# Attention weights that change partitions by DMA through a DRAM scratch instead of on GpSimd, and a bank of their own for block 0's scores

## The chip, the cores and the metric

One Trainium2 chip, and of it one core. The metric is the device time of one execution in microseconds; the number compared is the median over runs. TensorE (PE in profiles) multiplies matrices, VectorE (DVE), ScalarE (ACT) and GpSimd (POOL) do the elementwise work, and SyncE (SP) issues nearly all DMAs. PSUM, into which TensorE writes, has eight banks of 128 partitions x 512 f32.

## The reference

Windowed causal attention (8 batches, 8 heads, 576 positions, head size 64, window 64) gives 4608 tokens of 512 features; they go through an RMS norm and a gated MLP with 1536 hidden features.

```python
scores = scale * np.matmul(q, k.transpose(0, 1, 3, 2))
mask = (rel >= 0) & (rel < window)
scores = np.where(mask, scores, -1000000000.0)
attn = np.exp(scores - np.max(scores, axis=-1, keepdims=True))
attn = attn / (np.sum(attn, axis=-1, keepdims=True) + 1e-09)
x = (attn @ v).transpose(0, 2, 1, 3).reshape(4608, 512)
xn = x / np.sqrt(np.mean(x * x, axis=-1, keepdims=True) + 1e-06) * rms_g
g = xn @ w_gate
out = (g * sigmoid(g) * (xn @ w_val)) @ w_out
```

## The kernel before

Tokens are worked on in nine tiles of 512. The MLP's matmuls are in f16, each f32 operand split into a high and a low half, three matmuls for one product. Tiles 0 to 2 run plainly (`expert_in`, L794 to L796 and L843 to L846). Tiles 3 to 8 (`all_sevens`, L922) form a 2 x 2 block product from seven products instead of eight: for each of six chunks of hidden features the products 1, 5, 2, 6, 3, 7 and 4 stand at the slots of the table PLACE, 66 slots a tile, with output groups (six matmuls of L794 to L796 into a bank `po`) in slots that are free. Product 4 of a chunk adds into the bank of product 1, and so waits until VectorE has taken product 7's sum out of it (L982). Its weights come from a scratch in DRAM, `sevens`, through `load_sevens` (L895 to L904): three sets of four SBUF tiles `wt`, one set a chunk, loaded three chunks ahead as soon as the chunk that used the set is through its product 4. The sevens themselves are made during tiles 1 and 2 (L870 to L884, the halves `hi` and `lo` going out to DRAM over SP).

Attention is worked on by pairs of heads, n = 0 to 31, four a batch. Batches 0 and 1 turn their weights with matmuls. The 24 pairs from n = 8 on are spread over the MLP by `visit(n)`, whose places are numbers in half steps (32 a tile): the table VISITS for the first, then every 8. A visit does two things on TensorE. First come the scores of pair n (`quarter`, L389): nine blocks, eight of 128 columns into two banks `sc_n_0` and `sc_n_1`, and block 0, of 64 columns, into the tail (from column XSPLIT = 320) of a bank `x0_n`. Then come the values of pair n-2 (`attention_values`, L511): the first five blocks into columns 0 to 319 of that same bank `x0_n`, the other four into one more bank, `xp`.

The scores leave PSUM on VectorE: `masked` (L402), block 0 first, writes them with the mask added to the SBUF tile `pm_n` and keeps their extreme in `st_n`; ScalarE takes the exponentials (`weigh`, L405) and the sums; VectorE forms the reciprocals (L431, L432). The weights must then be turned so that keys lie on partitions. That takes two steps. POOL's `move` (L374) carries 32-row blocks between groups of partitions and multiplies by the reciprocal on the way, 16 instructions a pair, in four parts that are due 4 to 8.7 half steps after the visit and 0.8 apart (MOVES); VectorE's `turn` (L377, L378) transposes the 32 x 32 blocks, due three half steps before visit n+2. Two tiles' halves of `pm_n` serve as source and target. In the same time the values of finished pairs are squared and summed (L579), and at the end of a batch normalised: inverse roots on VectorE (L692 to L699), scaling (L744), splitting into halves on ACT and POOL (L777, L778, with VectorE's L783 to L789).

What sets the order: TensorE's order is that of the program from tile 1 on. The other engines' queues, SP's among them, are put in order by a scheduler when the kernel is built, on a timeline that it estimates; on the chip each queue then runs strictly in order. After tile 2 all eight banks of PSUM are handed out in rotation (`any_bank`); before that block 0's bank comes from a small pool.

## Time and profile before

| | |
|---|---|
| median of 3 runs | 1045.39 us (1043.51 to 1045.95) |
| the profiled execution | 1047.58 us |
| its span, first to last instruction | 1045.8 us |
| mean granted clock of TensorE | 0.97 |
| busy: PE, DVE, ACT, POOL | 975.9, 668.9, 510.6, 543.1 us |
| TensorE's first instruction of tile 1, 2, 3, 4 | 210.97, 348.2, 459.0, 561.5 us |
| visits' scores of pairs 18, 22, 26, 30 | 447.7, 550.2, 656.6, 762.0 us |
| DMA bytes | 143.42 MB |

Rows of the profile read: line, engine, operation, tiles out<-in, count, busy us, then the idle time ahead of them and what ended it. A wait row gives the line that waited and the line that released it, the us in all, the times and the longest. A timeline row begins with the start in us from the span's start and the duration.

### The profile page before, as it was taken

How to read it: one execution, taken by the hardware profiler on the slowest of the kernel's cores; microseconds unless marked ns; L12 is line 12 of the kernel's file. 1: busy time of each engine (PE TensorE's matmuls, PEld its weight loads, DVE VectorE, ACT ScalarE, POOL GpSimd, SP SyncE). 2: the span in 40 equal slices, each digit the busy share in tenths (PEclk: the TensorE clock that was granted, in tenths of full speed). 3: DMA queues.
4: the chain of work that ended last, by engine and by line, in shares of the span. 5: the costliest groups of instructions: out<-in, count | busy, mean ns of one | idle time of the engine just before them, and what ended most of it. 6: DMA issues, size and time to landing. Idle time of an engine off the chain costs nothing.

```text
span 1045.8 us, 20545 instructions
## 1 busy us (share of the span) xinstructions
PE 975.9 (93%) x7751; PEld 632.9 (61%) x7751; DVE 668.9 (64%) x1713; ACT 510.6 (49%) x1303; POOL 543.1 (52%) x679
## 2 busy tenths in 40 slices
PE   7889989998978999989998999899989999999998
PEld 5544544543433454468755885588558847866875
DVE  5688956377869744856686668666876666531550
ACT  5557885254522444256535654565346525532541
POOL 3326633579866666766666666666666404200210
PEclk9989989999989899999998999999999999999999
DMA  7647961222220444136632664266325523641501
GB/s 284 193 139 216 269 187 46 76 95 97 88 86 30 157 141 144 55 97 217 210 114 87 218 204 138 87 213 206 130 75 179 177 89 96 207 152 54 189 2 41
DMA packets 71331, 143.42 MB, mean 137 GB/s; under 512 B 25024, under 2 KB 25280, under 8 KB 71232
## 3 DMA queue, kind: packets, MB, share of 16 engines
q1 hardware_dynamic: 70656, 140.93, 42.3%
q8 instruction: 61, 1.00, 0.4%
q10 hardware_dynamic: 576, 1.18, 0.3%
q14 instruction: 38, 0.31, 0.1%
HBM read 121.64 MB, written 20.45 MB: 136 GB/s over the span
## 4 chain that ended last, share of the span: by engine, by line
PE 58%; DVE 18%; POOL 12%; ACT 7%; issue 3%; DMA 2%; SPq 0%; POOLq 0%; DVEq 0%; ACTq 0%
PE a L922 26%; POOL pm L374 10%; PE po L794 6%; PE po L795 6%; PE po L796 6%; DVE xb L744 3%; PE sc L389 2%; ACT pm L405 2%; DVE r L697 2%; DVE r L698 2%; PE xp L511 2%; DVE r L699 2%; PE x L511 2%; DVE pm L377 1%; PE pv L794 1%
## 5 line engine op out<-in xcount | busy, mean ns | idle before, releaser
L374 POOL TENSOR_TENSOR pm<-pm,st 32x288 f32<-32x288 f32 (+1 forms) x384 | 267.8, 697 | 115.1 <-DVE st L432 45.6
L922 PEld LDWEIGHTS <-wt 128*128 128x128 f16 x3024 | 295.8, 98 | 42.9 <-issue 2.2
L922 PE MATMUL a<-xn,wt 128*128 128x256 f16 x1728 | 203.8, 274 | 1.2 <-ACT ot L1041 0.8
L795 PE MATMUL po<-wt,h 128*128 128x512 f16 (+1 forms) x436 | 165.0, 378 | 0.0
L794 PE MATMUL po<-wt,h 128*128 128x512 f16 (+1 forms) x436 | 164.7, 378 | 0.0
L796 PE MATMUL po<-wt,h 128*128 128x512 f16 (+1 forms) x436 | 164.6, 378 | 0.0
L954 POOL TENSOR_TENSOR h<-th,h 128x512 f16<-128x512 f32 x60 | 69.1, 1159 | 154.5 <-ACT h L953 139.3
L922 PE MATMUL a<-wt,wt 128*128 128x256 f16 x1224 | 146.2, 273 | 0.0
L405 ACT ACTIVATE pm<-pm,st 128x128 f32<-128x128 f32 (+1 forms) x216 | 83.2, 387 | 21.8 <-DVE st L402 21.6
L947 DVE SCALAR_TENSOR_TENSOR th<-th,a 128x256 f32<-128x256 f32 x108 | 45.3, 419 | 65.1 <-ACT th L946 65.0
L946 ACT ACTIVATE th<-a,hsc 128x256 f32<-128x256 f32 x108 | 51.3, 475 | 52.6 <-PE a L922 29.8
L953 ACT CAST h<-th 128x512 f16<-128x512 f32 x72 | 44.4, 617 | 63.4 <-DVE th L948 63.4
L796 PEld LDWEIGHTS <-h 128*128 128x128 f16 x436 | 43.1, 99 | 49.4 <-issue 2.2
L794 PEld LDWEIGHTS <-h 128*128 128x128 f16 x436 | 43.3, 99 | 46.9 <-issue 3.0
L795 PEld LDWEIGHTS <-h 128*128 128x128 f16 x436 | 43.1, 99 | 46.0 <-issue 3.4
L794 PE MATMUL pv<-xn,wt 128*128 128x512 f16 x144 | 57.6, 400 | 8.9 <-DVE th L843 8.9
L389 PE MATMUL sc<-kv,q 64*64 64x128 f32 (+1 forms) x1056 | 56.5, 296 | 8.1 <-DMA q<-q 5.1
L777 ACT CAST xn<-xb 128x192 f16<-128x192 f32 (+7 forms) x33 | 12.9, 423 | 101.7 <-DVE xb L744 101.5
L377 DVE STREAM_TRANSPOSE pm<-pm 128x1024 f32<-128x1024 f32 x24 | 29.8, 1243 | 48.1 <-POOL pm L374 48.1
L975 DVE TENSOR_TENSOR a<-a,s 128x512 f32<-128x512 f32 x36 | 25.0, 696 | 54.7 <-PE a L922 54.6
L778 POOL TENSOR_TENSOR xn<-xb,xn 128x192 f16<-128x192 f32 (+7 forms) x33 | 28.3, 877 | 58.1 <-ACT xn L777 57.7
L511 PE MATMUL x<-pm,kv 128*64 128x64 f32 (+1 forms) x480 | 26.1, 250 | 34.7 <-DVE st L402 34.7
(184 smaller groups left out, 1831.2 us busy)
## 6 DMA issues: line engine op xcount, KB each, us to landing
wt<-sevens SPq DMA_DIRECT2D x108, 512.0 KB, 3.8
kv<-kv SPq DMA_DIRECT2D x28, 608.0 KB, 4.7
wt<-sevens SPq DMA_DIRECT2D x36, 256.0 KB, 3.7
q<-q SPq DMA_DIRECT2D x28, 288.0 KB, 3.0
kv<-kv SPq DMA_DIRECT2D x56, 128.0 KB, 4.8
out<-ot SPq DMA_DIRECT2D x27, 256.0 KB, 2.0
st<-w_gate SPq DMA_DIRECT2D x6, 1024.0 KB, 6.4
st<-w_val SPq DMA_DIRECT2D x6, 1024.0 KB, 5.9
```

The lines of the kernel that those rows point to most:

```text
L374: nc.gpsimd.tensor_tensor(m[to, :us, fr], p[fr, :us, to], r, ALU.mult)
L389: nc.tensor.matmul(out.rearrange("p (n c) -> p n c", c=D), lhsT=qt[hd, j * D : (j + 1) * D], rhs=halves[hd, :1, :] if j == 0 else halves[h ...
L405: nc.scalar.activation(part, part, AF.Exp, bias=low, scale=-1.0, accum_out=total)
L511: nc.tensor.matmul(xp[hd, c * D : (c + 1) * D], lhsT=vv[j][rows, hd], rhs=w, start=True, stop=True, skip_group_check=True,)
L794: nc.tensor.matmul(acc, lhsT=lh, rhs=rh, start=first, stop=False)
L795: nc.tensor.matmul(acc, lhsT=lh, rhs=rl, start=False, stop=False)
L796: nc.tensor.matmul(acc, lhsT=ll, rhs=rh, start=False, stop=last)
L922: nc.tensor.matmul(acc[:, i * HT : (i + 1) * HT], lhsT=ws[l][:, kt, :], rhs=b[:, m, kt, :], start=at_start, stop=kt == 1 and j == 2, skip_ ...
L946: nc.scalar.activation(cols, acc[:, :HT], AF.Tanh, scale=th_scale[:, c : c + 1])
L947: nc.vector.scalar_tensor_tensor(cols, cols, 1.0, acc[:, :HT], ALU.add, ALU.mult)
L953: nc.scalar.copy(hh, th)
L954: (nc.vector if c == NC - 1 else nc.gpsimd).tensor_tensor(hl, th, hh, ALU.subtract)
```

## The change

It has three parts. Block 0's scores get a bank `s0_n` of their own; in tiles 0 to 2 it comes from the pool with one bank that other small results use too. The move between partitions leaves POOL: for a pair, two multiplies over all 128 partitions by the reciprocals (128 x 1024 and 128 x 64), a memset, then on SP four DMA writes of 144 KB, one for each group of 32 partitions, into a scratch `via` in DRAM, and one read of 576 KB back into the other half of `pm_n`. For this the weights lie as [partition, 32-column block k, key block j, 32]. The moves are due 1.5 half steps after the visit and the transposes 6. Last, `load_sevens` loads a chunk's weights with two DMAs (1024 and 768 KB) in place of four, and two small buffers lose their second copy to make room.

```diff
@@ -40,13 +40,13 @@
 VISITS = (27, 32, 37, 42.5, 47.5)
-MOVES = (8.7, 7, 4.5, 4)
+MOVED, TURNED = 1.5, 6
 FIRST7 = 3
 PREP0, PREP1 = 34.0, 72.0
-ST = 2 * NBLK * P - D
+ST = 2 * NBLK * P - 32
 NRB = 2
@@ -101,7 +101,8 @@
-    wt = [cp.tile([P, 2, 1024], F16, name=f"wt{i}") for i in range(3 * NC + 2)]
+    wts = [cp.tile([P, 4, 2, 1024], F16, name=f"wt{i}") for i in range((3 * NC + 2) // 4)]
+    wt = [w[:, i] for w in wts for i in range(4)]
@@ -359,23 +360,29 @@
         t = wk.tile([P, ST], I32, tag="st8", name=f"pm_{n}", bufs=NST).bitcast(F32)
-        return (t[:, a : a + NBLK * P].rearrange("p (j k) -> p j k", k=P) for a in (0, ST - NBLK * P))
+        return (t[:, a : a + NBLK * P].rearrange("p (k j c) -> p k j c", k=4, j=NBLK) for a in (0, ST - NBLK * P))
-    def move(m, p, rs, k):
-
-        us = NBLK - 1 if k > 1 else NBLK
+    def move(n, m, p, rs):
+
+        for ks, us in ((4, slice(0, NBLK - 1)), (2, slice(NBLK - 1, NBLK))):
+            r = rs[:, us].rearrange("p (a j b) -> p a j b", a=1, b=1).to_broadcast([P, ks, us.stop - us.start, 32])
+            nc.gpsimd.tensor_tensor(p[:, :ks, us, :], p[:, :ks, us, :], r, ALU.mult)
+        nc.gpsimd.memset(p[:, 2:, NBLK - 1, :], 0.0)
+        via = dram.tile([P, 4, NBLK * 32], F32, tag="via", name=f"via_{n}", bufs=3)
         for qq in range(4):
-            fr, to = slice(32 * qq, 32 * qq + 32), slice(32 * k, 32 * k + 32)
-            r = rs[fr, :us].rearrange("p (a b) -> p a b", b=1).to_broadcast([32, us, 32])
-            nc.gpsimd.tensor_tensor(m[to, :us, fr], p[fr, :us, to], r, ALU.mult)
+            nc.sync.dma_start(
+                out=via[:, qq, :].rearrange("(k i) c -> i k c", k=4),
+                in_=p[32 * qq : 32 * qq + 32].rearrange("i k j c -> i k (j c)"),
+            )
+        nc.sync.dma_start(out=m.rearrange("p q j c -> p q (j c)"), in_=via)
     def turn(p, m):
-        nc.vector.transpose(p[:, : NBLK - 1, :], m[:, : NBLK - 1, :])
-        nc.vector.transpose(p[0:D, NBLK - 1, :], m[0:D, NBLK - 1, :])
+        nc.vector.transpose(p[:, :, : NBLK - 1, :], m[:, :, : NBLK - 1, :])
+        nc.vector.transpose(p[0:D, :, NBLK - 1, :], m[0:D, :, NBLK - 1, :])
@@ -423,11 +430,12 @@
             w, v = P if u else D, slot(u)
-            masked(p[:, v, :w], place[u] if u else first[:, :D], blocked[:, :P] if u else blocked[:, P:],
-                   st[:, 0, v : v + 1])
+            src, hide = (x.rearrange("p (k c) -> p k c", c=32) for x in (
+                (place[u], blocked[:, :P]) if u else (first[:, :D], blocked[:, P:])))
+            masked(p[:, : w // 32, v, :], src, hide, st[:, 0, v : v + 1])
         for u in order:
             w, v = P if u else D, slot(u)
-            weigh(p[:, v, :w], st[:, 0, v : v + 1], st[:, 1, v : v + 1])
+            weigh(p[:, : w // 32, v, :], st[:, 0, v : v + 1], st[:, 1, v : v + 1])
         nc.vector.tensor_scalar(st[:, 1, :], st[:, 1, :], 1e-9, None, ALU.add)
@@ -507,9 +515,10 @@
                 i, par = divmod(j - 1 - 4 * g, 2)
-                w = at(1 + 4 * g + 2 * h + i)[:, par * D : (par + 1) * D] if j else at(0)[rows, hd]
+                w = at(1 + 4 * g + 2 * h + i, rows, par) if j else at(0, rows, h)
+                o = xp[hd, c * D : (c + 1) * D]
                 nc.tensor.matmul(
-                    xp[hd, c * D : (c + 1) * D],
+                    o if len(w.shape) == 2 else o.rearrange("p (a b) -> p a b", b=32),
                     lhsT=vv[j][rows, hd],
@@ -538,9 +547,9 @@
-        def moved(hp, k):
+        def moved(hp):
             p, m, rs = whole[b * NPAIR + hp]
-            move(m, p, rs, k)
+            move(b * NPAIR + hp, m, p, rs)
@@ -556,9 +565,9 @@
                 place = {u: p[h][:, i, :] for h in range(2) for i, u in enumerate(units(g, h))}
-                at = place.get
+                at = lambda u, rows, a: place[u][rows, a * D : (a + 1) * D]
             else:
-                at = lambda u: p[:, slot(u), :]
+                at = lambda u, rows, a: p[rows, 2 * a : 2 * a + 2, slot(u), :]
             xp = attention_values(n, g, at, vv, xp)
@@ -597,9 +606,8 @@
                 events.append((i0 - 7, partial(load_keys, hp)))
-                for k in range(4):
-                    events.append((i0 + (MOVES[hp] + 0.8 * k if n > 11 else 3.5 + 0.4 * k), partial(moved, hp, k)))
-                events.append((visit_at(n + 2) - half_steps * (b - 1) - 3, partial(turned, hp)))
+                events.append((i0 + MOVED, partial(moved, hp)))
+                events.append((i0 + TURNED, partial(turned, hp)))
                 visits[n] = partial(score, hp, 0), partial(values, hp)
@@ -623,7 +631,7 @@
         if n in visits:
-            visits[n][0](xp[:, XSPLIT:])
+            visits[n][0](any_bank(f"s0_{n}") if shared else ps_mi.tile([P, TT], F32, tag="mi", name=f"s0_{n}"))
         if n - 2 in visits:
@@ -896,12 +904,9 @@
             return
-        src = sevens[r % NC]
-        for j in range(4):
-            n = 2048 if j < 3 else 1024
-            nc.sync.dma_start(
-                out=wt[4 * (r % 3) + j].rearrange("p a n -> p (a n)")[:, :n], in_=src[:, 2048 * j : 2048 * j + n]
-            )
+        dst = wts[r % 3].rearrange("p i a n -> p (i a n)")
+        for a, z in ((0, 8 * TT), (8 * TT, 14 * TT)):
+            nc.sync.dma_start(out=dst[:, a:z], in_=sevens[r % NC][:, a:z])
```

What it moves on the queues is shown at three places. Lines of the changed kernel are 5 to 9 higher.

TensorE at visit 22, at the end of tile 3. `x_22` is the bank x0, `xp_1` the bank of the other values, `s_22` block 0's own bank, `sc_0` and `sc_1` the other scores, `po_3` an output group, `a_4_0` the first product of tile 4. Before:

```order
L389 MATMUL x_22_5748<-kv_5542,q_5540 64x64 x2
L389 MATMUL sc_0_5749<-kv_5542,q_5540 64x128
L389 MATMUL sc_1_5750<-kv_5542,q_5540 64x128
...
L511 MATMUL xp_1_5804<-pm_5152,kv_4873 64x64 x8
L794 LDWEIGHTS h_2_4758
L794 MATMUL po_3_5731<-wt_95,h_2_4758 128x512
...
L511 MATMUL x_22_5748<-pm_5152,kv_4873 64x64 x10
L794 LDWEIGHTS h_3_4948
L794 MATMUL po_3_5731<-wt_96,h_3_4948 128x512
```

And after:

```order
L396 MATMUL s_22_5642<-kv_5446,q_5444 64x64 x2
L396 MATMUL sc_0_5643<-kv_5446,q_5444 64x128
L396 MATMUL sc_1_5644<-kv_5446,q_5444 64x128
...
L520 MATMUL x_22_5641<-pm_5056,kv_4787 64x64 x10
L520 MATMUL xp_1_5698<-pm_5056,kv_4787 64x64 x8
...
L802 MATMUL po_3_5628<-wt_84,h_2_4671 128x512
...
L802 MATMUL po_3_5628<-wt_84,h_3_4869 128x512
```

The values into `x_22` moved ahead of `xp` and of one output group, directly behind the scores, and no longer write into a bank that holds scores. The later rows of TensorE are the same in both.

VectorE behind visit 22, at the first products of tile 4. `a_4_0` are the banks of those products, `th_0_0` and `th_0_1` the gate's tiles, `wt_92` and `wt_83` the tile into which product 7's sum is taken (L982, L987), `pm_5769` and `pm_5663` the weights of pair 22. Before:

```order
L432 RECIPROCAL st_5770<-st_5770 128x9
L975 TENSOR_TENSOR a_4_0_5877<-a_4_0_5877,s_4_0_5855 128x512
L947 SCALAR_TENSOR_TENSOR th_0_0_5891<-th_0_0_5891,a_4_0_5877 128x256
L948 SCALAR_TENSOR_TENSOR th_0_0_5891<-a_4_0_5877,th_0_0_5891 128x256
L978 TENSOR_TENSOR a_4_0_5863<-a_4_0_5863,s_4_0_5907 128x512
L947 SCALAR_TENSOR_TENSOR th_0_0_5891<-th_0_0_5891,a_4_0_5863 128x256
L948 SCALAR_TENSOR_TENSOR th_0_0_5891<-a_4_0_5863,th_0_0_5891 128x256
L982 TENSOR_TENSOR wt_92<-a_4_0_5842,wt_92 128x512
L377 STREAM_TRANSPOSE pm_5769<-pm_5769 128x1024
L947 SCALAR_TENSOR_TENSOR th_0_1_5965<-th_0_1_5965,wt_92 128x256
L378 STREAM_TRANSPOSE pm_5769<-pm_5769 64x128
```

And after:

```order
L440 RECIPROCAL st_5664<-st_5664 128x9
L980 TENSOR_TENSOR a_4_0_5772<-a_4_0_5772,s_4_0_5741 128x512
L952 SCALAR_TENSOR_TENSOR th_0_0_5786<-th_0_0_5786,a_4_0_5772 128x256
L953 SCALAR_TENSOR_TENSOR th_0_0_5786<-a_4_0_5772,th_0_0_5786 128x256
L983 TENSOR_TENSOR a_4_0_5749<-a_4_0_5749,s_4_0_5802 128x512
L384 STREAM_TRANSPOSE pm_5663<-pm_5663 128x4x256
L952 SCALAR_TENSOR_TENSOR th_0_0_5786<-th_0_0_5786,a_4_0_5749 128x256
L385 STREAM_TRANSPOSE pm_5663<-pm_5663 64x4x32
L953 SCALAR_TENSOR_TENSOR th_0_0_5786<-a_4_0_5749,th_0_0_5786 128x256
L987 TENSOR_TENSOR wt_83<-a_4_0_5728,wt_83 128x512
```

The two transposes of pair 22 moved ahead of the sum L987 (L982 before), by three rows.

SP around visit 24, inside tile 4. `wt` from `sevens` are weight loads, `kv` and `q` the inputs of later pairs. Before:

```order
L902 DMA wt_81<-sevens_143 128x2048
L902 DMA wt_82<-sevens_143 128x2048
L324 DMA q_7143<-q 128x576
L902 DMA wt_83<-sevens_143 128x2048
L902 DMA wt_84<-sevens_143 128x1024
L902 DMA wt_85<-sevens_144 128x2048
L902 DMA wt_86<-sevens_144 128x2048
L339 DMA kv_6545<-kv 128x1216
L352 DMA kv_6545<-kv 64x512
L353 DMA kv_6545<-kv 64x512
L902 DMA wt_87<-sevens_144 128x2048
L902 DMA wt_88<-sevens_144 128x1024
```

And after, with `via` the scratch and `pm_6334` the weights of pair 24:

```order
L909 DMA wt_81<-sevens_128 128x4096
L325 DMA q_6997<-q 128x576
L909 DMA wt_81<-sevens_128 128x3072
L377 DMA via_6473<-pm_6334 32x4x288 x3
L340 DMA kv_6413<-kv 128x1216
L353 DMA kv_6413<-kv 64x512
L354 DMA kv_6413<-kv 64x512
L377 DMA via_6473<-pm_6334 32x4x288
L909 DMA wt_82<-sevens_129 128x4096
L381 DMA pm_6334<-via_6473 128x1152
L909 DMA wt_82<-sevens_129 128x3072
```

The four writes wait for POOL's multiply and the read for the writes; what stands behind them in the queue is issued after them. A weight load waits for TensorE to be done with its tile, and one stands between the last write and the read.

More of the change, by code (lines that the diff above doesn't have):

```diff
@@ L296, in out_split @@
     def out_split():
-        mx = wk.tile([P, 1], F32, tag="mo1", name="omx")
+        mx = wk.tile([P, 1], F32, tag="mo1", name="omx", bufs=1)
         nc.vector.tensor_tensor(w_sq, w_sq, h_inv, ALU.mult)
@@ L684, in inverse_roots @@
             )
-        rm = wk.tile([P, 3, nst], F32, tag="rm", name=f"rm_{b}")
+        rm = wk.tile([P, 3, nst], F32, tag="rm", name=f"rm_{b}", bufs=1)
         m, r, w = (rm[:, i, :] for i in range(3))
```

## The prediction

> **What bounds the kernel now.** I read the page first, then the waits of TensorE by stage, the windows with the granted clock, the timeline round one visit, and last the DMA landings. The page's first row says that TensorE is the engine that sets the time; what it does not do is 7% of the span.
>
> ```profile
> PE 975.9 (93%) x7751; PEld 632.9 (61%) x7751; DVE 668.9 (64%) x1713; ACT 510.6 (49%) x1303; POOL 543.1 (52%) x679
> ```
>
> TensorE's waits, first from 211 to 346 us (tile 1), then from 346 to 880 us (tiles 2 to 6). Columns: total us, times, longest.
>
> ```profile
> PE x L511 <- DVE st L402: 14.5, 4, 6.9
> PE pv L794 <- DVE th L843: 6.1, 2, 3.9
> ...
> PE x L511 <- DVE st L402: 20.1, 9, 4.5
> ```
>
> Nearly all that TensorE waits for after 211 us is one thing: the values of pair n-2 (L511) go into the bank in which block 0's scores of pair n still stand, and VectorE's mask (L402) has not read them yet. Behind the long waits the granted clock falls. The windows give busy us of PE, PEld, DVE, ACT and POOL, then the clock; the first two rows are tile 1 and a later tile.
>
> ```profile
> 211.00:346.00 135.00, 114.31 (x787) 56.04 (x787) 108.74 (x257) 58.79 (x181) 100.13 (x114) 0.92 0.26 87
> 565.00:670.00 105.00, 99.57 (x942) 73.59 (x941) 73.19 (x195) 54.58 (x156) 67.22 (x90) 0.98 0.50 159
> ...
> 297.80:304.60 6.80, 5.24 (x31) 2.77 (x32) 5.31 (x26) 4.55 (x21) 0.00 (x0) 0.50 0.29 84
> 338.70:345.50 6.80, 4.68 (x40) 2.96 (x41) 5.69 (x25) 4.82 (x21) 1.16 (x1) 0.50 0.72 252
> 451.40:454.80 3.40, 3.40 (x39) 2.42 (x40) 1.55 (x16) 3.40 (x16) 1.55 (x3) 0.50 0.73 238
> 557.20:564.00 6.80, 6.49 (x38) 3.92 (x39) 4.95 (x25) 6.24 (x25) 4.83 (x7) 0.50 0.41 130
> 663.00:666.40 3.40, 3.33 (x25) 1.96 (x26) 3.40 (x17) 3.12 (x12) 3.40 (x4) 0.50 0.27 69
> 768.80:772.20 3.40, 3.40 (x25) 1.63 (x20) 3.37 (x17) 2.59 (x10) 3.40 (x4) 0.50 0.44 119
> 256.80:263.60 6.80, 5.14 (x13) 1.83 (x13) 5.70 (x9) 1.85 (x4) 5.99 (x8) 0.50 0.52 171
> ```
>
> Seven stretches at half clock: 20.4 us of them in tile 1 (three of 6.8), 17.0 us later (3.4 + 6.8 + 3.4 + 3.4). Half of each is lost work. So after 346 us 20.1 + 8.5 = 28.6 us hang on that bank, and in tile 1 14.5 + 6.1 + 10.2 = 30.8 us hang on VectorE being late (108.7 of 135 us busy there, against 73 of 105 later).
>
> **The change part by part: block 0's own bank.** It removes the wait at L511 itself. What is late next is read at visit 22, at the end of tile 3. Every tile end after 346 us has this form; the waits at the other three stand in the last rows.
>
> ```profile
> 532.19 0.21 DVE L432 RECIPROCAL st<-st 128x9 f32<-128x9 f32 x1
> 532.57 12.73 POOL L374 TENSOR_TENSOR pm<-pm,st 32x288 f32<-32x288 f32 x16 [8.61 <-ACT kv L574]
> 535.53 0.75 DVE L697 TENSOR_TENSOR r<-r 128x256 f32<-128x256 f32 x1
> 545.50 1.23 DVE L377 STREAM_TRANSPOSE pm<-pm 128x1024 f32<-128x1024 f32 x1
> 550.25 0.27 PE L389 MATMUL x<-kv,q 64*64 64x64 f32 x2
> 550.27 0.49 DVE L697 TENSOR_TENSOR r<-r 128x320 f32<-128x320 f32 x1
> 551.38 0.69 PE L511 MATMUL xp<-pm,kv 128*64 128x64 f32 x16
> 557.23 0.22 DVE L402 CUSTOM_DVE_ANT_0 pm<-x,blocked 128x64 f32<-128x64 f32 x1
> 557.51 1.53 PE L511 MATMUL x<-pm,kv 64*64 64x64 f32 x20 [4.04 <-DVE st L402]
> 561.51 2.70 PE L922 MATMUL a<-xn,wt 128*128 128x256 f16 x12
> 562.19 0.21 DVE L432 RECIPROCAL st<-st 128x9 f32<-128x9 f32 x1
> 565.34 1.47 PE L922 MATMUL a<-wt,wt 128*128 128x256 f16 x12
> 566.65 1.47 PE L922 MATMUL a<-xn,wt 128*128 128x256 f16 x12
> 576.05 1.25 DVE L377 STREAM_TRANSPOSE pm<-pm 128x1024 f32<-128x1024 f32 x1 [0.67 <-POOL pm L374]
> 578.42 3.77 PE L922 MATMUL a<-xn,wt 128*128 128x256 f16 x33
> ...
> 451.32 0.99 PE L511 MATMUL x<-pm,kv 64*64 64x64 f32 x10 [2.37 <-DVE st L402]
> 663.07 1.21 PE L511 MATMUL x<-pm,kv 64*64 64x64 f32 x14 [4.31 <-DVE st L402]
> 768.16 1.09 PE L511 MATMUL x<-pm,kv 64*64 64x64 f32 x20 [4.50 <-DVE st L402]
> ```
>
> Count from the scores, 550.25 = 0. With a bank of its own TensorE goes on: values at half of 1.53 us, the second bank's 0.6, two output groups of 1.3 (what lies between the first product of tile 4 and the one at 565.34 is one group, with a matmul's tail), so tile 4 begins at about +5.1 instead of +11.3. By the order its next gates are the bank of block 0's scores (second product, behind one more output group, +7.7; the mask is read at +7.2) and sc's bank (+9.0, when four masks of 0.2 us are done too). They are met almost without a wait. The five shorter waits after 346 us (20.1 less 2.37, 4.04, 4.31 and 4.50 at the tile ends, so 4.9 us) go for good: **-4.9**.
>
> **POOL's moves become DMAs.** Removed are 384 moves, added two multiplies per pair over all partitions.
>
> ```profile
> L374 POOL TENSOR_TENSOR pm<-pm,st 32x288 f32<-32x288 f32 (+1 forms) x384 | 267.8, 697 | 115.1 <-DVE st L432 45.6
> L233 POOL TENSOR_TENSOR wt<-wt,wt 128x1024 f16<-128x1024 f32 x7 | 16.7, 2391 | 2.5 <-ACT wt L232 1.6 <-DVE wt L232 0.7
> ```
>
> 16 x 0.697 = 11.2 us of POOL per pair become, with the 128x1024 row as the nearest for the large multiply, 2.4 + 0.2 + some 0.1 for the memset, 2.7 us (up to 1024/288 x 0.697 + 0.2 = 2.7). VectorE gains too: its 128x256 step took 0.75 us while POOL moved and the larger 128x320 step 0.49 once POOL stood still, so 0.39 for 256 columns. The nine such steps and the following normalisation ahead of visit 22 lose some 4.5 us; but the transposes behind them now wait for a read, and what is left of the 4.5 at the masks is about 2.5 us.
>
> **The way through the scratch.** New per pair are four writes of 144 KB and one read of 576 KB, on SP's queue, in order. The trace has no such trip; the nearest landings and issue costs:
>
> ```profile
> sevens<-hi SPq DMA_DIRECT2D x12, 256.0 KB, 2.0
> sevens<-wt SPq DMA_DIRECT2D x24, 128.0 KB, 4.0
> wt<-sevens SPq DMA_DIRECT2D x108, 512.0 KB, 3.8
> kv<-kv SPq DMA_DIRECT2D x28, 608.0 KB, 4.7
> ...
> 549.72 1.30 SPq L1054 DMA_DIRECT2D out<-ot  x3
> ```
>
> An issue costs 0.43, so the fourth write goes 1.3 us after the first; it lands 2.0 to 4.0 later (I take 2.0, a write out of SBUF with pieces over 1 KB), the read 3.8 to 4.7 (I take 4.4, between the two by size). From the reciprocal: 0.2 + 2.7 + 1.3 + 2.0 + 4.4 = 10.6 us, against 12.9 for POOL's moves at visit 21 (532.40 to 545.30). So it is quicker than POOL by 2.3 us; with the ends of the rows it is 10.0 to 12.9.
>
> But the transposes stand earlier now: at visit 22 ahead of the sum that frees product 4 of the tile's first chunk, where before they stood behind it. Reciprocal at +9.7 (562.40 less 2.5), read landed at +20.3, then transpose 1.25, three steps of about 0.4 and the sum of 0.7, so the bank is free at +23.5. TensorE stands at product 4 at 5.1 + 16.9 (561.51 to 578.42) less 1.3 of half clock = +20.7. **A new wait of 2.8 us** (2.2 to 5.1 by the landings, 7.6 if VectorE gains none of the 2.5 us as well), and behind a wait of that size the clock fell for 3.4 us at 451.40, 1.7 us more. Four tile ends give up 15.2 + 8.5 = 23.7 us and take back 4 x 4.5 = 18.0: **-5.7**, with ends of -23.7 (no wait at product 4) and +13.5 (four waits of 7.6 and 1.7).
>
> A rule of the Trainium skill would have these new waits cheaper. The row first: the wait of 2.37 us (451.32, above) was followed by 3.4 us at 0.50, a wait of 2.27 us ahead of 234.45 by none of the seven stretches.
>
> ```profile
> 234.45 0.38 PE L794 MATMUL pv<-xn,wt 128*128 128x512 f16 x1 [2.27 <-DVE th L843]
> ```
>
> The page "TensorE: Matmul & The Clock Gate" of the Trainium skill, section on the HAM clock gate, has the clock fall only after a whole idle window of about 3.4 us, counted freely; by that the four waits would cost 11 and not 18 us, and the time would be 1010. The trace disagrees for 2.37 us, so I keep 1.7 us each.
>
> At the visits inside a tile the transposes stand within a few rows of their old place, and VectorE waited there for POOL already (row below, 2.5 us each time), so data that come no later cost nothing.
>
> **Tile 1.** 30.8 us hang on VectorE there. POOL is busy 100.1 of the 135 us; five pairs less at 8.5 us each free 42 us of it, and VectorE's steps on SBUF get shorter as above. An estimate: by the pair 0.75 and 0.39 such a step is 1.9 times as long under POOL, and POOL is busy 74% of the tile now and would be some 45%; if half of VectorE's 108.7 us are such steps, 54 us of them become 54 x 1.41/1.67 = 46, 8 less, and the bank takes its 14.5 us of waits away directly. VectorE keeps 100 us of work in an order that does not change, so I choose a little over half of the 30.8, **-18**; the bounds are 5 (the bank's waits come back behind VectorE's other rows) and 31.
>
> **The rest, at nothing.** Four weight loads a chunk become two of 1024 and 768 KB: their lead is about eight products of 1.31 us (565.34 to 566.65), 10.5 us, over a landing of perhaps 6 (an estimate from 3.8 for 512 KB); a load that comes without that cover would cost TensorE up to those 6. Masks, exponentials and values read pieces of 32: between -0.1 and +0.2 us a pair on VectorE, which has idle time. Blocks in five banks a visit, not four: met by the gates above.
>
> **Sum:** -4.9 - 5.7 - 18 = -28.6. The profiled execution took 1047.58 us, which becomes 1019.0; the median of the runs is 2.2 us lower at 1045.39, so **1016.8**, say 1017.
>
> **The rivals.**
> *The reads land in time.* Write 2.0, read 3.8 and a reciprocal as early as VectorE could have it: no wait at product 4. Then 4.9 + 23.7 + 18 to 31 = 47 to 60 us, **986 to 999**. For it: TensorE has 15 us of its own work before product 4. Against: the chain above. Chance 0.22.
>
> *The waits only change their place.* The reads come 3 us later than I say, so the tile ends give nothing or a little back, and tile 1, where SP's queue also holds the writes of the prepared weights that free VectorE's buffers, gains only 5 to 12: **1030 to 1045**. For it: VectorE's order is fixed, and so is SP's. Chance 0.15, a third of it within 0.2% (2 us, about what a measurement of this kernel tells from no change).
>
> *Slower: the read is held in SP's queue.* At visits 19, 20, 23 and 24 a weight load stands between the last write and the read, and it waits for a product to free its tile. Those come four products apart, 5.2 us. Held so long, the read is 5 us late, VectorE stands before a sum that TensorE needs, and about 2 us a visit come through. The point from which it decides is 28.6/24 = 1.2 us a visit; at 2 us and 20 visits it is 40 - 28.6 = 11 us over: **1057**. For it: the order. Against: VectorE waited at the transposes before, by this row for POOL, 19 times and 48.1 us in all, and TensorE's waits name none of it as lasting after tile 1.
>
> ```profile
> DVE pm L377 <- POOL pm L374: 48.1, 19, 5.2
> ```
>
> The page "DMA: Bandwidth & Descriptors" of the Trainium skill, section on the anatomy of one DMA, says that the wait sits on the issuing sequencer and DMA engines only consume their queues, which is this mechanism; no run here shows its price yet. Chance 0.10.
>
> **How the numbers follow.** My forecast 0.53 (1003 to 1030), the rivals 0.22, 0.15, 0.10. Faster by over 0.2%: 0.53 + 0.22 + 0.10 = 0.85; within: 0.05; slower: 0.10. The range leaves out the slow rival, the upper end of the second and the deeper half of the first: 995 to 1040.
>
> **What would show it.** Right: no wait at the values' line; the first transpose of a tile-end visit waits for a DMA, and behind it TensorE waits 2 to 5 us at a product L927; tile 1 ends near 330 us instead of 348; POOL falls from 543 to about 340 us; the trip from reciprocal to landed read takes 10 to 11 us. Wrong: waits on weight loads; waits at L927 at visits inside a tile; VectorE's short steps no shorter; or no wait at all at the tile ends, then it is the first rival.

## The result, and the profile after

The changed kernel took 1055.2 us (median of 4, 1054.1 to 1056.1) against 1045.3 for the kernel before: ratio 1.0097, 95% interval 1.0080 to 1.0115. The forecast was 1017, with up to 1040 in its range: the sign is wrong. The profiled execution has a span of 1054.3 us, 8.5 more than before, at a mean granted clock of 0.97, as before.

The page's first row of the changed kernel:

```profile
PE 972.0 (92%) x7740; PEld 629.6 (60%) x7751; DVE 655.8 (62%) x1713; ACT 507.1 (48%) x1303; POOL 338.6 (32%) x367
```

POOL has lost 204.5 us of work, as forecast. TensorE's busy time is 3.9 us lower and the span 8.5 longer: what has grown, by some 12.4 us, is the time in which it waits. TensorE's waits over the whole span, changed kernel first, then the one before (line that waited, line that released it, us in all, times, longest):

```profile
PE pv L802 <- DVE th L851: 14.4, 8, 5.4
PE a L927 <- ACT s L942: 9.3, 3, 3.6
PE tot L712 <- DVE ssq L588: 8.2, 4, 4.8
PE a L927 <- ACT wt L942: 7.9, 7, 3.1
PE a L927 <- DVE wt L987: 6.0, 4, 3.0
...
PE a L927 <- ACT ot L1046: 3.2, 1, 3.2
PE pg L802 <- DVE th L852: 3.1, 2, 1.8
...
PE a L927 <- DVE st L409: 2.5, 3, 1.3
...
PE pg L802 <- ACT wt L239: 1.6, 1, 1.6
```

```profile
PE x L511 <- DVE st L402: 34.7, 13, 6.9
PE pv L794 <- DVE th L843: 8.9, 5, 3.9
...
PE pg L794 <- ACT wt L238: 1.8, 1, 1.8
...
PE a L922 <- ACT ot L1041: 0.8, 1, 0.8
...
PE a L922 <- ACT wt L937: 0.4, 1, 0.4
```

The 34.7 us at the values' line are gone altogether. In their place stand 28.9 us at the products (L927, the five rows; 1.2 before), 8.2 at the sums of squares (no such row before), 14.4 instead of 8.9 at `pv` and 4.7 instead of 1.8 at `pg`: 44.3 us more against 34.7 less. With the small rows that are not shown, all of TensorE's waits come to 78.2 us where there were 65.7, as much more as the span's growth (8.5) and the fall of busy time (3.9) together. So the gain did not fail to come at the bank; it was given back at other gates.

By stage: visit 14's scores, at the end of tile 1, came 1.4 us earlier than before (332.2 for 333.6), and TensorE's last matmul ended 8.9 us later (1050.9 for 1042.0). So 10.3 us were lost behind tile 1, where the forecast had a gain of 10.6.

Tile 1 of the changed kernel (busy us of PE, PEld, DVE, ACT, POOL, then the clock), the row that answers to the first window of before:

```profile
211.00:346.00 135.00, 121.64 (x856) 59.06 (x853) 110.98 (x269) 59.99 (x186) 55.90 (x55) 0.95 0.44 136
```

POOL fell from 100 to 56 us there, yet VectorE is as full as it was (111.0 against 108.7).

**Where the gain went, at one place.** VectorE ahead of visit 26, in the middle of a batch's normalisation: the last of the inverse roots, the scaling, and the transposes of pair 25. Before:

```profile
644.94 0.71 DVE L699 SCALAR_TENSOR_TENSOR r<-r,r 128x192 f32<-128x192 f32 x1
...
647.76 2.72 DVE L744 SCALAR_TENSOR_TENSOR xb<-xb,gsb,r 128x192 f32<-128x192 f32 x4
...
652.35 1.23 DVE L377 STREAM_TRANSPOSE pm<-pm 128x1024 f32<-128x1024 f32 x1
```

After:

```profile
644.92 0.36 DVE L707 SCALAR_TENSOR_TENSOR r<-r,r 128x192 f32<-128x192 f32 x1
645.31 1.41 DVE L752 SCALAR_TENSOR_TENSOR xb<-xb,gsb,r 128x192 f32<-128x192 f32 x4
...
652.32 1.25 DVE L384 STREAM_TRANSPOSE pm<-pm 128x1024 f32<-128x1024 f32 x1 [4.97 <-DMA pm<-via]
```

VectorE's steps beside a free POOL take half as long, as forecast, and the scaling ends at 646.7 instead of 650.5. Then VectorE stands 4.97 us before transposes whose data have not landed, and starts them at 652.32, where before it started them at 652.35. All of the gain is in that wait. What follows on ScalarE and TensorE at visit 26, before:

```profile
661.85 0.51 ACT L777 CAST xn<-xb 128x384 f16<-128x384 f32 x1 [7.40 <-DVE xb L744]
...
670.37 0.58 ACT L937 COPY s<-a 128x512 f32<-128x512 f32 x1
```

After:

```profile
662.67 0.51 ACT L785 CAST xn<-xb 128x384 f16<-128x384 f32 x1 [6.62 <-DVE xb L752]
...
668.07 0.39 ACT L412 ACTIVATE pm<-pm,st 128x128 f32<-128x128 f32 x1
...
670.81 0.58 ACT L942 COPY s<-a 128x512 f32<-128x512 f32 x1
...
671.44 1.89 PE L927 MATMUL a<-wt,wt 128*128 128x256 f16 x12 [3.41 <-ACT s L942]
```

ScalarE waits for VectorE's scaled rows, is then full with casts (L785) and exponentials (L412), and behind those in its queue stands the copy (L942) that frees a bank for a product: at 670.81, before at 670.37. TensorE no longer waits 4.31 us at the values; it waits 3.41 us at that product.

**The trip inside a tile.** Visit 27 of the changed kernel, scores at 689.1: the reciprocal, POOL's multiply, the four writes, the read, the transposes.

```profile
695.19 0.21 DVE L440 RECIPROCAL st<-st 128x9 f32<-128x9 f32 x1
695.54 2.47 POOL L373 TENSOR_TENSOR pm<-pm,st 128x1024 f32<-128x1024 f32 x2 [2.95 <-DVE st L440]
698.04 1.29 SPq L377 DMA_DIRECT2D via<-pm  x3
...
701.01 0.58 SPq L377 DMA_DIRECT2D via<-pm  x1
701.69 1.38 SPq L909 DMA_DIRECT2D wt<-sevens  x2
705.47 0.32 SPq L381 DMA_DIRECT2D pm<-via  x1
...
711.91 1.25 DVE L384 STREAM_TRANSPOSE pm<-pm 128x1024 f32<-128x1024 f32 x1 [1.92 <-DMA pm<-via]
```

From the reciprocal's end at 695.40 it takes 2.6 us to the end of the multiplies, 3.0 to the fourth write (three loads of keys are issued in between), 4.5 until the read is issued, 6.4 until the transposes start on it: 16.5 us, where the forecast had 10.6. Where nothing stands in between, at the ends of tiles, it is near the forecast: 11.3, 11.4 and 11.8 us at visits 22, 26 and 30, between the same events. At the other visits from 19 on it is 13.0 to 17.0, while in the kernel before, where VectorE waited for POOL at these visits, the transposes began 12.9 to 13.3 us behind the reciprocal. The read itself is not held up by the weight loads ahead of it: in all 24 trips it was issued at most 0.14 us after the last write had landed, and SP waited at most 0.58 us for TensorE at a load in between. VectorE's idle time at the transposes, in groups by line (the last two figures), with 48.1 us before:

```profile
L384 DVE STREAM_TRANSPOSE pm<-pm 128x1024 f32<-128x1024 f32 x24 | 29.9, 1245 | 72.5 <-DMA pm<-via 60.3
```

### The profile page after: what moved, and what is told of

Its sections match the earlier page's. It is cut to its first block, busy times and chain, and to the rows that moved or that the text cites. A ratio compares the mean times of both kernels' runs of the same rounds, so it can differ in the third digit from the quotient of the medians.

```text
span 1054.3 us, 20343 instructions
## 1 busy us (share of the span) xinstructions
PE 972.0 (92%) x7740; PEld 629.6 (60%) x7751; DVE 655.8 (62%) x1713; ACT 507.1 (48%) x1303; POOL 338.6 (32%) x367
## 4 chain that ended last, share of the span: by engine, by line
PE 29%; DMA 11%; DVE 10%; ACT 9%; issue 3%; POOL 3%; SPq 2%; DVEq 0%; ACTq 0%; POOLq 0%
PE a L927 17%; DMA pm<-via 6%; DMA via<-pm 5%; ACT pm L412 5%; PE po L802 4%; PE po L804 4%; PE po L803 4%; POOL pm L373 2%; DVE pm L384 2%; SPq L377 1%; DVE th L952 1%; DVE th L953 1%; ACT h L958 1%; ACT th L951 1%; DVE xb L752 1%
## 5 line engine op out<-in xcount | busy, mean ns | idle before, releaser
L927 PEld LDWEIGHTS <-wt 128*128 128x128 f16 x3024 | 297.2, 98 | 75.3 <-issue 32.9
L927 PE MATMUL a<-xn,wt 128*128 128x256 f16 x1728 | 206.3, 275 | 19.7 <-ACT wt L942 7.9
L959 POOL TENSOR_TENSOR h<-th,h 128x512 f16<-128x512 f32 x60 | 69.6, 1160 | 249.2 <-ACT h L958 241.7
L927 PE MATMUL a<-wt,wt 128*128 128x256 f16 x1104 | 134.9, 275 | 9.3 <-ACT s L942 9.3
L412 ACT ACTIVATE pm<-pm,st 128x128 f32<-128x128 f32 (+1 forms) x216 | 83.1, 387 | 24.3 <-DVE st L409 24.1
L373 POOL TENSOR_TENSOR pm<-pm,st 128x1024 f32<-128x1024 f32 (+1 forms) x48 | 59.2, 1252 | 88.0 <-DVE st L440 59.0
L384 DVE STREAM_TRANSPOSE pm<-pm 128x1024 f32<-128x1024 f32 x24 | 29.9, 1245 | 72.5 <-DMA pm<-via 60.3
L802 PE MATMUL pv<-xn,wt 128*128 128x512 f16 x144 | 57.6, 400 | 14.4 <-DVE th L851 14.4
L803 PEld LDWEIGHTS <-wt 128*128 128x128 f16 x296 | 29.6, 100 | 54.3 <-issue 24.1
L854 POOL TENSOR_TENSOR h<-th,h 128x512 f16<-128x512 f32 x30 | 37.4, 1251 | 69.5 <-ACT h L853 60.5
L802 PE MATMUL pg<-xn,wt 128*128 128x512 f16 x144 | 54.8, 381 | 5.3 <-DVE th L852 3.1
L785 ACT CAST xn<-xb 128x192 f16<-128x192 f32 (+7 forms) x33 | 12.9, 423 | 96.4 <-DVE xb L752 96.2
```

The source lines that it names most:

```text
L373: nc.gpsimd.tensor_tensor(p[:, :ks, us, :], p[:, :ks, us, :], r, ALU.mult)
L384: nc.vector.transpose(p[:, :, : NBLK - 1, :], m[:, :, : NBLK - 1, :])
L412: nc.scalar.activation(part, part, AF.Exp, bias=low, scale=-1.0, accum_out=total)
L802: nc.tensor.matmul(acc, lhsT=lh, rhs=rh, start=first, stop=False)
L803: nc.tensor.matmul(acc, lhsT=lh, rhs=rl, start=False, stop=False)
L927: nc.tensor.matmul(acc[:, i * HT : (i + 1) * HT], lhsT=ws[l][:, kt, :], rhs=b[:, m, kt, :], start=at_start, stop=kt == 1 and j == 2, skip_ ...
```

## The experiments

Fifteen kernels, in four groups. The expectations name the theories by letter. **A**: the transposes stand in VectorE's order ahead of their data; VectorE works in order, so all that is queued behind (masks, scaling, the sums that free banks) comes late. **B**: the bank removes a wait whose cause stays, so it comes back at the next gate. **C**: the trip itself costs, by its traffic or by holding SP's queue. Later A is taken apart by where the wait stands. All ratios are against the kernel before.

**The bank.** e1_own_bank is the kernel before with this one line:

```diff
-            visits[n][0](xp[:, XSPLIT:])
+            visits[n][0](any_bank(f"s0_{n}") if shared else ps_mi.tile([P, TT], F32, tag="mi", name=f"s0_{n}"))
```

> The kernel before with block 0's scores in a bank of their own and nothing else. If the way through the scratch is what costs (theory A), the bank by itself is good: the 34.7 us of waits at the values' line go, and the time is 1015 to 1030. If the bank only moves the wait (theory B), TensorE goes past the values and stops 2 to 4 us at product 6 of the tile's first chunk, whose bank ScalarE copies only after the visit's exponentials; then the time is 1035 to 1045. Either way no wait at the values' line.

Measured: 1042.6 us, 0.9975 (0.9964 to 0.9985). Its waits:

```profile
PE a L922 <- ACT s L937: 10.9, 3, 3.9
```

With POOL's moves untouched TensorE stops at tile ends with ScalarE's copy as the gate, as in the changed kernel: this wait needs no trip, it stands behind the values' wait that the bank removes. Of 34.7 us of waits, 2.7 us of time are gained. B holds for the bank.

e2_no_own_bank is the reverse, the changed kernel with block 0's scores back in the tail of `x0`.

> The changed kernel with block 0's scores back in the tail of the values' bank. Theory A: the waits at the values' line come back on top of the transposes' waits, 1060 to 1075. Theory B: the wait goes back to where it was, and the time stays within 5 us of the changed kernel, 1050 to 1060.

Measured: 1063.0 us, 1.0163 (1.0146 to 1.0180), inside the range of theory A. The row of old is back, on top of VectorE's waits for the read (62.9 us):

```profile
PE x L520 <- DVE st L409: 33.9, 11, 7.2
```

Beside the late transposes the bank is worth 7.8 us.

**The trip's cost.** e3_no_trip leaves the exchange between partitions out: POOL's multiply writes where the transposes read, and there is no DMA.

```diff
-            nc.gpsimd.tensor_tensor(p[:, :ks, us, :], p[:, :ks, us, :], r, ALU.mult)
...
+            nc.gpsimd.tensor_tensor(m[:, :ks, us, :], p[:, :ks, us, :], r, ALU.mult)
...
```

> The changed kernel without the DMAs through the scratch: GpSimd's multiply writes the second half of the tile and the transposes read that, so 32-row blocks stay in their partitions (that part of the computation is left out). Everything else of the change stays. The transposes are free about 3 us after the reciprocal, in place of 11 to 17. Theory A: VectorE's 72 us of waiting at the transposes fall under 15 and the time to 1015 to 1030. Theory B: the tile ends still stop at product 6, 1040 to 1050.

Measured: 1006.2 us, 0.9625 (0.9608 to 0.9641), below the range of either theory. 49 us hang on the trip in some way, though the scheduler put the transposes 2 to 20 rows earlier in VectorE's queue than in the changed kernel. e4_trip_unused puts the five DMAs back and uses nothing that they carry (the read goes to a second scratch); the second transpose still overlaps the written columns and so waits for the writes.

```diff
...
-                in_=p[32 * qq : 32 * qq + 32].rearrange("i k j c -> i k (j c)"),
+                in_=m[32 * qq : 32 * qq + 32].rearrange("i k j c -> i k (j c)"),
...
-        nc.sync.dma_start(out=m.rearrange("p q j c -> p q (j c)"), in_=via)
...
+        nc.sync.dma_start(out=back, in_=via)
```

> As the run without the trip, but the four writes to the scratch are issued as in the changed kernel, and 576 KB are read from it again, into a second scratch in DRAM; nobody waits for them but SP's queue and the reuse of the buffers. (The same part of the computation is left out.) If the cost is that VectorE waits for the data (theory A), this is within 5 us of the run without the trip. If it is the traffic, or what SP's queue holds back (theory C), it is at 1045 to 1060 like the changed kernel, and TensorE waits on weight loads or inputs.

Measured: 1029.4 us, 0.9837 (0.9815 to 0.9858), in neither range, because of that wait; with it ScalarE's copy is late at the tile ends again:

```profile
DVE pm L386 <- DMA via<-pm: 36.7, 22, 4.1
...
PE a L928 <- ACT s L943: 8.6, 3, 3.9
```

e5_trip_unused takes that overlap away (writes of 128 KB from `m[..., 1:, :]`, a read of 512 KB).

> The run with the unused trip again, since there the second transpose wrote 32 columns that the writes to the scratch still read, and so waited for them. Now the writes leave those columns out (128 KB each, and 512 KB read), and no engine waits for a DMA of the trip. (The same part of the computation is left out.) Theory A, the cost is the waiting alone: 1004 to 1012, like the run without the trip. Theory C, SP's held queue and the traffic cost as such: 1020 or more, and the waits of TensorE and VectorE name loads.

Measured: 1005.3 us, 0.9605 (0.9590 to 0.9620). SP is held at the read as in the changed kernel, here e5 and then the changed kernel:

```profile
SPq L382 <- DMA via<-pm: 61.2, 33, 4.9
```

```profile
SPq L381 <- DMA via<-pm: 57.8, 35, 4.1
```

The transfers, their issue and the held queue cost nothing: e5 is no slower than e3. C falls. Between e4 and e5, whose transfers differ by a ninth of their bytes, stand one group of VectorE's waits, 36.7 us in all, and 24 us of time: A. This is the cleanest pair of all, since every engine has the same order in both but for a few rows that are one or two places off, and the late copy on ScalarE (8.6 us) is gone with VectorE's waits.

e7_pool_queue issues the five DMAs from GpSimd's queue, past the loads.

```diff
-            nc.sync.dma_start(
+            nc.gpsimd.dma_start(
...
-        nc.sync.dma_start(out=m.rearrange("p q j c -> p q (j c)"), in_=via)
+        nc.gpsimd.dma_start(out=m.rearrange("p q j c -> p q (j c)"), in_=via)
```

> The changed kernel with the trip's five DMAs issued on GpSimd's queue, directly behind the multiply. Nothing of SP's queue stands between the last write and the read, and SP is not held. If the loads between them are what makes the trip 14 to 17 us inside a tile in place of 11 (theory C), the trip is 9 to 12 us at every visit and the time 1030 to 1045; if the place of the transposes is what counts (theory A), the gain is what the shorter trip gives VectorE, some 20 of its 72 us, and the time 1040 to 1052. Against it stands that GpSimd's own rows wait behind the read.

Measured: 1050.1 us, 1.0041 (1.0022 to 1.0060), in the range of theory A. But the trip became no shorter: from visit 19 on it is 13.8 to 20.2 us, for POOL is busy 67 us more, all of it with issuing the DMAs. VectorE's waits for the read fall only to 47.7 us. So this run says little about the loads between the writes. e8_four_loads loads a chunk's weights with four DMAs again, in slices of the same tile.

> The changed kernel with a chunk's weights loaded by four DMAs again, nothing else. By every theory the loads have no part in it: within 5 us of the changed kernel, 1050 to 1060, unless the 1024 KB loads between the last write and the read are what lengthens the trip; then the trip is 2 us shorter inside a tile and the time 1040 to 1050.

Measured: 1058.3 us, 1.0128 (1.0099 to 1.0157), the trip as long as in the changed kernel (11.1 to 17.4 us from visit 19 on): that the loads are larger has no part in it.

**The place of the transposes.** e6_turn_later makes them due at 9 half steps, and ties them to the VectorE instruction that stands ahead of them in the program, so that they cannot be put earlier by the scheduler's estimate.

```diff
...
-MOVED, TURNED = 1.5, 6
+MOVED, TURNED = 1.5, 9
...
-            turn(p, m)
+            last = next(x for x in reversed(nc.cur_bb.bb.instructions) if x.engine == nc.vector.engine)
+            with tc.issue_after(last):
+                turn(p, m)
```

> The changed kernel with the transposes due 9 half steps after the visit in place of 6 and tied behind the vector instruction ahead of them in the program, so that they stand behind the next visit's reciprocal at most places, some 15 us later on VectorE, and the read has landed. Theory A: VectorE's 60 us of waiting for the read fall under 10, and the time falls to 1010 to 1025. Theory C: the waits go but the time stays over 1030.

Measured: 1008.8 us, 0.9645 (0.9625 to 0.9664), the fastest that leaves nothing out, 36.5 us below the result's median of the kernel before. The trip is as long as ever inside tiles (17.5 us from the reciprocal to the landed read at visit 27); VectorE waits for no read:

```profile
L384 DVE STREAM_TRANSPOSE pm<-pm 128x1024 f32<-128x1024 f32 x24 | 29.5, 1231 | 0.0
```

e9_turn_later_no_bank is e6 with block 0's scores back in `x0`.

> The run with the later transposes, with block 0's scores back in the tail of the values' bank. If the bank has a worth of its own once VectorE is free, the waits at the values' line come back at the tile ends: 1018 to 1035. If VectorE's lateness was all there was to those waits, they stay under 8 us in all and the time within 4 us of the run with the bank, 1005 to 1013.

Measured: 1010.3 us, 0.9658 (0.9631 to 0.9685). The values' line waits 3.6 us for the mask, not 34.7 (and 2.9 for the transposes): once VectorE is on time, the bank is worth nothing that these runs can tell.

e12_turn_tied keeps the due time of 6 and adds only the tie.

> The changed kernel with its transposes tied to their place in the program at 6 half steps, as in the changed kernel, not 9: they stand up to a dozen rows later than in the changed kernel, and still ahead of the next visit. If it is how late they stand that counts, part of the gain: VectorE waits 20 to 50 us for the read, and 1020 to 1048. If the tie as such did it (the order of the other rows that it brings), 1005 to 1013.

Measured: 1012.6 us, 0.9673 (0.9648 to 0.9698). Its waits, VectorE's at the transposes and TensorE's at the product of the three tile ends:

```profile
DVE pm L384 <- DMA pm<-via: 9.6, 6, 2.5
...
PE a L929 <- ACT s L944: 2.0, 3, 1.0
```

The tie brings 42.6 us. By the traces the transposes stand 18 to 39 rows later for the second pair of a batch, which moved from the middle of the normalisation to behind its scaling; 24 to 29 rows later for pairs 8, 10 and 11; 5 to 9 for ten pairs; and at most one for the other five. The time lies outside A's range (1020 to 1048) and inside that of the other theory, the order of the other rows that the tie brings. Other rows did move: at the three tile ends six of VectorE's rows that make the next tile's operands (L792, L794, L797) stand 6 to 16 rows earlier, and the casts that they feed moved ahead of exponentials on ScalarE. So e12 alone can't part the waits at the transposes from those rows; e4 and e5, with the same order and 24 us apart, show that the waits alone can cost such a sum. To tell the two kinds of place apart, e14_tied_hp1 ties only the second pairs (9, 13, ... 29) and e15_tied_others only the others.

```diff
...
+                if hp == 1:
+                    last = next(x for x in reversed(nc.cur_bb.bb.instructions) if x.engine == nc.vector.engine)
+                    order.enter_context(tc.issue_after(last))
...
```

> The changed kernel with only the second pair of each batch (9, 13, 17, 21, 25, 29) tied to its place at 6 half steps: from pair 13 on their transposes leave the middle of the batch's normalisation on VectorE and stand 20 to 36 rows later, behind it; the others stay where they are, and VectorE goes on waiting some 2 to 5 us for the read at each of them. Theory A1, what counts is the wait in the middle of the normalisation, on which the tile's end hangs: 1015 to 1035. Theory A2, each wait counts alike: 5 of 19 waits go, and 1042 to 1050.

> The counterpart: all pairs but the second of each batch are tied at 6 half steps and stand 0 to 9 rows later, the second ones stay in the middle of the normalisation. Theory A1: 1035 to 1052, and the waits at the tile ends stay. Theory A2: 14 of 19 waits are shortened or gone, 1018 to 1032.

Measured: 1040.9 us, 0.9962 (0.9943 to 0.9981), and 1032.0 us, 0.9865 (0.9851 to 0.9880): 14.3 and 23.2 below the changed kernel, 37.5 together of e12's 42.6. Their waits, e14 and then e15:

```profile
PE a L931 <- DVE wt L991: 11.7, 6, 2.8
...
PE a L931 <- ACT s L946: 2.0, 3, 1.0
```

```profile
PE a L931 <- ACT s L946: 8.8, 3, 3.3
```

Each has one gate cleared and the other left. Where the second pairs are tied, ScalarE's copy is late by 2.0 us in place of 8.8; the six rows of VectorE at the tile ends have moved there too, so that this run does not tell which of the two cleared it (e4 and e5 do it by the wait alone). The other pairs' transposes delay VectorE's sum that frees product 4 (11.7 us where they are not tied, no such row where they are), and those rows did not move in e15. So both kinds of place cost.

**POOL's way with the transposes elsewhere.** e10_before_turn_later ties them in the kernel before at their old due time, three half steps ahead of visit n+2; e11_bank_turn_later adds the bank.

> The kernel before, GpSimd's moves and the shared bank kept, with only its transposes tied behind the vector instruction ahead of them in the program (three half steps before visit n+2), some 15 us later on VectorE than the scheduler put them. If a transpose that stands too early is the fault of both kernels (theory A), VectorE's 48 us of waiting for GpSimd fall under 10 and the time to 1025 to 1038. If it is the scratch alone that needs it, the time stays at 1041 to 1048.

> The kernel before with the bank of its own and the later transposes, the moves still on GpSimd. If freeing GpSimd is worth nothing by itself, it is as good as the later transposes on the changed kernel, 1005 to 1013. If VectorE's and ScalarE's chain at the tile ends is long because GpSimd slows VectorE, the wait at product 6 stays, and it is 1018 to 1035.

Measured: 1063.9 us, 1.0170 (1.0146 to 1.0194), and 1060.1 us, 1.0124 (1.0097 to 1.0152). Both expectations were missed, since the tie put the transposes too late, as this row of e10 shows: the values wait for them.

```profile
PE xp L511 <- DVE pm L377: 38.8, 4, 11.8
```

They tell nothing of POOL. e13_bank_turn_tied ties them too, but makes them due right behind POOL's last move, with the bank; of its edit only the due time is shown:

```diff
...
-                events.append((visit_at(n + 2) - half_steps * (b - 1) - 3, partial(turned, hp)))
+                events.append((i0 + (MOVES[hp] + 2.6 if n > 11 else 4.9), partial(turned, hp)))
...
```

> The kernel before with the bank of its own and GpSimd's moves, the transposes tied to a place right behind the last part of the move (2.6 half steps behind its first part), so that neither kernel's mistake is in it: not ahead of its data and not as late as the next values. If the place of the transposes was all, and the way of the move has no part in it: 1005 to 1018. If GpSimd's freedom counts as well: 1025 to 1045, with ScalarE's and VectorE's lateness at the tile ends still in TensorE's waits.

Measured: 1036.8 us, 0.9914 (0.9899 to 0.9929). VectorE waits there 7.0 us for POOL, none of it after pair 11, but ScalarE's copy is late all the same. The cause of that is not shown:

```profile
PE a L924 <- ACT s L939: 11.0, 3, 3.9
...
DVE pm L377 <- POOL pm L374: 7.0, 3, 2.5
```

From pair 12 on the transposes of a batch's first two pairs start 18 to 28 us after POOL's last move had ended, so for these the place is far behind the data. The four kernels with the bank, in us (e13's and e12's due times differ, each set for its own way):

| | transposes where the scheduler put them | tied behind their data |
|---|---|---|
| POOL's moves | 1042.6 (e1) | 1036.8 (e13) |
| way through the scratch | 1055.2 (the change) | 1012.6 (e12) |

The kernel with the scratch is 24 us faster with the transposes tied, and 13 slower with them where the scheduler put them. How much of the 24 is the way itself, and how much the place, is not shown. Across the kernels with that way or its remains, the time follows VectorE's idle time at the transposes (us, all causes):

| | e6 | e12 | e3 | e5 | e15 | e4 | e7 | e14 | change |
|---|---|---|---|---|---|---|---|---|---|
| idle at the transposes | 0 | 13.0 | 13.6 | 13.6 | 35.5 | 50.3 | 52.3 | 59.5 | 72.5 |
| time | 1008.8 | 1012.6 | 1006.2 | 1005.3 | 1032.0 | 1029.4 | 1050.1 | 1040.9 | 1055.2 |

The first 14 us cost little: in e3 and e5 they are waits for POOL, and those two are no slower than e6; e12, with 13.0, is 3.8 us slower than e6. From there to the change it is (1055.2 - 1006)/(72.5 - 13.6) = 0.8 us of time for each us; e4, e15 and e7 lie 7 to 12 us off that line, so what stands behind a wait matters too.

## Why the prediction was wrong

**The step that failed** is "data that come no later cost nothing" at the visits inside a tile, priced at zero for most of the 24 pairs. It failed twice over. First, VectorE came sooner, as the same forecast said, so data of the same hour became a longer wait: 4.97 us at pair 25, no wait there before. VectorE's gain of 3.8 us there passed no further than its next wait for something that had not become faster. Second, the data did come later at most visits inside tiles: 13.0 to 17.0 us behind the reciprocal, not 10.6, by the loads issued between the writes and by slower landings among them (4.5 and 6.4 us at visit 27). VectorE's waits at the transposes so became 72.5 us for 48.1. e4 and e5 put a price on such waits, 24 us for 36.7; e12, which clears all but 13.0 of the 72.5 by the place, gains 42.6, with the other rows that its tie moved.

**"They are met almost without a wait"** failed too, for the gates behind the bank. Only VectorE's masks and the banks were checked. The copy on ScalarE that frees a bank for a product stands behind a visit's casts and exponentials; it came at 670.81, as late as ever. The bank alone brought 2.7 us (e1), not the 28.6 that the forecast hung on it behind tile 1.

The other steps:
- Values' wait gone: right, 34.7 to 0. The term -4.9 for the five in-tile waits can't be seen by itself.
- POOL to about 340 us, VectorE's steps half as long: right (338.6; 0.71 to 0.36). Multiply and the rest for 2.7 us a pair: 2.47 and a memset of 0.15.
- The trip at tile ends, 10.6 us: right within 1.2. A wait of 2.8 at product 4 of each tile end: seen once there, 1.45 us behind visit 22; the two others over 1 us, 3.01 and 1.16, came behind visits 20 and 28, inside tiles, which was named as a sign against the forecast.
- Tile 1, -18: visit 14's scores came at 332.2 instead of 333.6, 1.4 earlier. VectorE waited 3.0 and 3.6 us for the reads of pairs 12 and 13 there. With the waits gone (e6) they came at 322.0, 11.6 earlier: the mechanism is there, and the size still two thirds of the forecast's.
- Weight loads, masks in pieces, five banks, at nothing: nothing speaks against it (e8).
- Half clock behind every new wait, 1.7 us: by the last section, not behind every one. Of the waits behind visit 22 (2.24, 1.45 and 1.25 us) none had it.

**The rivals.** The slow one (1057) gave nearly the time, by half its mechanism: late reads in front of a sum that TensorE needs. That its number fits is luck in part. Its cause, the read held behind a weight load, is not in the trace, where the read left at most 0.14 us after the writes had landed, and it named the sums alone, not the normalisation. The one in which waits only change their place saw the tile ends rightly, and still left too much of the gain in tile 1 (5 to 12 us for a measured 1.4). The fast one, "no wait at product 4", is what e6 and e12 come near to, with 36.5 and 32.7 us of gain for its 47 to 60. Behind visit 14 e6 gained 27.4 us (its last matmul ends 39.0 earlier, less the 11.6), near that rival's 28.6; the missing part is tile 1.

A rule of the Trainium skill was cited for the slow rival: the page "DMA: Bandwidth & Descriptors", section on the anatomy of one DMA, puts a DMA's wait on the issuing sequencer. The trace agrees that SP waits (57.8 us at the read), but that price is zero here (e5, 61.2 us of it).

## What to carry to other kernels

Before pricing a producer that becomes faster or a way that becomes longer, look where its consumer stands in the queue of an engine that works in order: a wait there is paid by all that is queued behind it, and tying the consumers to a place up to 39 rows later was worth 42.6 us here, more than the 28.6 that the whole change was forecast to bring. When a wait at one gate goes, follow every engine to the next gate, the copies on ScalarE among them, and ask which of them was late for the same cause. To price a long transfer, issue it and use nothing that it brings.

## What the runs showed of the hardware

The changed kernel moves 28.3 MB more than the one before (171.7 MB against 143.4). In e5, 25.2 MB more than in e3 (168.6 against 143.4) slowed nothing: 1005.3 us for 1006.2. The landings of the changed kernel (KB each, median us):

```profile
via<-pm SPq DMA_DIRECT2D x96, 144.0 KB, 2.8
pm<-via SPq DMA_DIRECT2D x24, 576.0 KB, 4.2
```

The clock behind a wait: first a wait of 3.01 us in the changed kernel, then one of 1.62 us in e12 and one of 3.14 us in e15, each with a window that follows it (the clock is the third figure from the end):

```profile
524.25 1.49 PE L927 MATMUL a<-xn,wt 128*128 128x256 f16 x12 [3.01 <-DVE wt L987]
...
526.00:527.00 1.00, 1.00 (x27) 1.00 (x23) 0.78 (x4) 0.69 (x3) 0.00 (x0) 0.50 0.59 78
```

```profile
483.51 2.50 PE L929 MATMUL a<-xn,wt 128*128 128x256 f16 x12 [1.62 <-DVE st L409]
...
483.90:487.10 3.20, 3.20 (x17) 2.27 (x16) 2.28 (x17) 3.20 (x16) 0.00 (x0) 0.50 0.00 1
```

```profile
658.29 1.47 PE L931 MATMUL a<-wt,wt 128*128 128x256 f16 x12 [3.14 <-ACT s L946]
...
658.50:662.00 3.50, 3.50 (x29) 2.55 (x27) 1.32 (x3) 2.44 (x5) 1.68 (x3) 1.00 0.49 110
```

In the changed kernel the waits of 3.0 to 3.6 us were followed by a stretch at half clock in all five cases, and so was the one of 2.37 before; those of 2.24 and 2.27 were not. But 1.62 us brought half clock in e12 and 3.14 us did not in e15, so the length of a wait does not decide by itself. In each of these runs the stretches last 3.4 or 6.8 us and begin whole multiples of 3.41 us apart, as on a grid, and what fits is the idle time of TensorE within one field of that grid. The field ahead of the fall held 2.09 us of it in the changed kernel (from 522.16) and 2.02 in e12 (from 480.36), there with a second wait of 0.40 us. In e15 the border between two fields cut the wait of 3.14 us into 1.65 and 1.49, and the wait of 2.24 lies as 0.68 and 1.56. Over all 17 kernels, among the fields at full clock from 200 us on (the last 20 us aside), the clock fell behind none with less than 0.52 of it idle, and behind every one with more than 0.58.

The Trainium skill's page "TensorE: Matmul & The Clock Gate", section on the HAM clock gate, asks for a whole idle window of some 3.4 us. The trace agrees with the length of the window, but 2.02 us of idle time within one were enough here, so the page is a little too mild, as the forecast's 1.7 us for every wait was too harsh.
